# Token blocks 2 and 3 transposed on VectorE and turned through DRAM instead of on TensorE

## Chip, cores and metric

The kernel runs on one core of a Trainium2 chip. The metric is the device time of one execution in microseconds (us); the kernel before has a median of 676.11 us over three runs. Everything is float32 outside and float32r (a float32 that TensorE takes) inside, where each operand is split in a high part and the low part that the high one leaves over, and a product is summed from high x high, high x low and low x high.

## What is computed

One layer on 2048 tokens of 448 values: a layer norm, then an attention with a memory that is carried over four blocks of 512 tokens, and a gated feed-forward, both on the normalised tokens; the result is the input plus both.

```python
def _A_ref(x, wq, wk, wv, wo, beta):          # H = 16 heads of 28, N = 4 blocks of L = 512
    q, k, v = ...                             # x @ wq, x @ wk, x @ wv by heads and blocks
    for s in range(N):
        logits = jnp.einsum("bhqd,bhkd->bhqk", qs, ks) * scale + mask
        a_dot = jnp.einsum("bhqk,bhkd->bhqd", _softmax(logits), vs)
        pq = phi(qs)                          # phi(t) = t + 1 if t > 0 else exp(t)
        num = jnp.einsum("bhld,bhde->bhle", pq, M)
        den = jnp.einsum("bhld,bhd->bhl", pq, z)[..., None] + 1e-6
        outs.append(g * num / den + (1.0 - g) * a_dot)
        M = M + jnp.einsum("bhld,bhle->bhde", phi(ks), vs)
        z = z + jnp.einsum("bhld->bhd", phi(ks))
    return o @ wo

def _B_ref(x, w_gate, w_up, w_down):
    return (_sigmoid(x @ w_gate) * (x @ w_up)) @ w_down

xn = _layernorm(x)
return x + _A_ref(xn, ...) + _B_ref(xn, ...)
```

## The kernel before

The work has two stages. The **front stage** (up to about 125 us, with an overlap to 155 us) loads the four blocks of 512 tokens, normalises them, turns them so that the 448 values lie on the partitions, and computes values, keys, queries and the memory of each block. The **main stage** runs the feed-forward over 14 slices of hidden width, two at a time over all four blocks, with the attention's scores, softmax and sums woven in, and at the end the output projection. In the front stage the orders of TensorE (PE), ScalarE (ACT) and VectorE (DVE) are as the code is written; the orders of the DMA queue of SyncE (SP) and of GpSimd (POOL) are set by a scheduler. In the main stage all five are as written. Each queue is in order: what stands behind a waiting instruction waits too.

The names that matter. `acc[b]` holds the input of block b (128 tokens on the partitions, four tiles of 448): the normalisation reads it, and the main stage adds its results to it, so it is also the residual. `xs[b]` is the turned and split block, seven groups of 512 columns: groups 0 to 2 the high parts, 4 to 6 the low parts of the first 384 values, and group 3 the remaining 64 values, high in partitions 0 to 63 and low in 64 to 127. `wqk[c]` are seven chunks of the weights of keys and queries.

For each block b the loop (from `for b in range(NB)`) does this:

- **values**: four tiles `pv` of 11 matmuls (L360), copied by ScalarE to `vst` (L364), and stored to DRAM as `vd`. Behind the first tile VectorE computes the statistics of block b + 1 (L319 and on), and behind the fourth it normalises the first two tiles of that block into `xn` (L345).
- **seven chunks** of keys and queries (`keys_queries`, k = 0 to 6): 11 matmuls into the bank `pp` (L380); ScalarE copies the high part to `qk` (L381) and makes `e` from `pp` (L385, L386); VectorE makes the low part (L387) and finishes `e` (L390); SP stores `qk` to `qd` and, for queries, `e` to `fd`. Two chunks later `key_rows` transposes `e` on TensorE (`pk`, L400) into `kn`.
- **the turn of block b + 1**, a tile of 128 tokens at a time behind chunks 1 to 4 (`turn`): four transposes on TensorE into a bank `pt` (L103), the high part by ScalarE (L105), the low by VectorE (L110, L111). The other two tiles are normalised there too.
- from b = 2 on, **the recall of block b - 1**: behind the first chunk (the second in the last block) 16 small matmuls into four banks `n2` (L433), four transposes on VectorE (L439), and behind each of the next four chunks an answer: four steps on VectorE that end in the transpose into `tb` (L444), and a store from POOL's queue (`od<-tb`, L445). `tb` has two buffers.
- **update**: the memory `mst` from `kn` and `vst` (`pmm`, L411), behind the seventh chunk.

The blocks of input are loaded by SP: 0 and 1 at the start, 2 and 3 behind a chunk's store of the blocks 0 and 1 (L582). In the last block TensorE's queue mixes in the first feed-forward matmuls (`pgu`, L255). At the start of the main stage come the last recall's answers, the loads of the scores' operands (`qk<-qd`), of the unit's values (`vv`), of the weights (`raw`, which ScalarE and VectorE split into `wgu`, L93 and L94), and the additions of the down projection's banks `pd` (L181) to `acc` (L183).

Of the kernel before, what the change touches and what calls it, by code (L numbers as in the profile page):

```python
# [9 lines left out]
F32 = mybir.dt.float32  # L10
# [59 lines left out]
def kernel(  # L70
# [45 lines left out]
    def x_block(b):  # L116
        return x[b * L:(b + 1) * L, :].rearrange("(t p) d -> p t d", p=P)

    ps = ctx.enter_context(tc.tile_pool(name="psum", bufs=1, space=PSUM))
# [29 lines left out]
    vd = [dram.tile([P, NT, H * 32], F32, name=f"vd{b}") for b in range(NB)]  # L149
    od = [dram.tile([H * 32, L], F32, name=f"od{b}") for b in range(NB)]  # L150
# [23 lines left out]
    def gated():  # L174
# [49 lines left out]
        for f0 in range(0, NF, FG):  # L224
# [3 lines left out]
            if f0 == 0:  # L228
                ahead[0, 0] = lambda: (load_down(1, "raw"), ready_up(1))
                ahead[0, 2] = lambda: load_up(2)  # L230
                ahead[1, 3] = lambda: load_up(3)
# [70 lines left out]
    with tc.tile_pool(name="front", bufs=2) as sb, tc.manual_schedule(engines=FRONT):  # L302
# [40 lines left out]
        def normalise(b, t, mean, y):  # L343
# [4 lines left out]
            if b == 0:  # L348
                A.activation(xn[:, D:], xn[:, 384:D], AF.Copy)
            else:  # L350
                G.tensor_copy(xn[:, D:], xn[:, 384:D])
            return xn

# [19 lines left out]
        stored = {}  # L373

        def keys_queries(b, c):
# [12 lines left out]
            stored[b, c] = nc.sync.dma_start(qd[b][c * P:(c + 1) * P], qk.bitcast(F32)).ins  # L388
            if e is not None:
# [47 lines left out]
        def turn_back(n2, ts):  # L437
            for i in range(NG):
                V.transpose(ts[:, i, :], n2[i])  # L439
# [97 lines left out]
        for b in range(NB):  # L537
            last = b == NB - 1
            xn = {}
# [17 lines left out]
            if st and b > 0:  # L557
                st = rstd(*st)
                for n in range(2):
                    xn[n] = normalise(b + 1, n, *st[n])  # L560
            e = {}
            for k, c in enumerate((3, 4, 5, 6, 0, 1, 2) if last else range(7)):
                e[c] = keys_queries(b, c)
                if b == 0 and c + 4 < 7:
                    split_qk(c + 4)
                n = k - (1 if last else 0)
                if b > 1 and n == 0:
                    ts = kn if last else phi
                    turn_back(recall(b - 1, phi), ts)
# [10 lines left out]
                if (b, k) in ((0, 3), (1, 0)):  # L580
                    with tc.issue_after(stored[b, c]):
                        nc.sync.dma_start(acc[b + 2], x_block(b + 2))  # L582
# [18 lines left out]
                n = k - 1 if b == 0 else k + 1  # L601
                if 2 <= n < 6:
                    turn(b + 1, n - 2, xn[n - 2])
                if 0 <= n < 4 and n not in xn:
                    xn[n] = normalise(b + 1, n, *st[n])
# [298 lines left out]
```

## Time and profile before

| | us |
|---|---|
| runs | 676.11, 676.07, 677.15 |
| median | 676.11 |
| the profiled execution | 676.94 |
| its span, first to last instruction | 675.1 |
| TensorE, wait for VectorE in front of `pt` | 1.3 |
| TensorE, wait in front of `pp` | 0.9 |
| TensorE, wait in front of `pv` | 0.8 |

The profiled execution is 1.8 us longer than its span and 0.8 us longer than the median. Rows of a timeline show the start, the duration, the engine, the line of the program, the operation with what it writes and reads, and, in brackets, the time for which the engine had sat idle before it and what ended that. Neighbouring instructions of one kind are merged in a row (x11). A matmul's row overlaps the next one's, so the pace of TensorE is read from start to start.

### The profile page before, as it was taken

What the parts mean: (1) busy time and instruction counts of PE and PEld (TensorE: products, weight loads), DVE (VectorE), ACT (ScalarE), POOL (GpSimd) and SP (SyncE); (2) the same over time, 40 slices, a digit from 0 to 9 for tenths busy, and PEclk for the clock granted to TensorE, in tenths of its full rate; (3) what the DMA queues carried; (4) which work ended last, traced back from release to release, by engine and by line L of the source; (5) the groups of instructions that cost most, each with busy time, mean ns of one, the idle gap of its engine ahead of it and who ended that gap; (6) DMA issues with size and microseconds to landing.
All of it is one profiled execution on the core that took longest, in us unless ns stands there. A gap on an engine that the chain in (4) does not pass through costs nothing.

```text
span 675.1 us, 11208 instructions
## 1 busy us (share of the span) xinstructions
PE 666.7 (99%) x3954; PEld 555.1 (82%) x3954; DVE 566.2 (84%) x987; ACT 338.5 (50%) x563; POOL 141.4 (21%) x346
## 2 busy tenths in 40 slices
PE   8999999999999999999999999999999999999998
PEld 7888878778888788787887878788787887888897
DVE  6765685668989899899999889899998998999864
ACT  4846574523554564555644454465545554544320
POOL 3500010002222222142221213222222221321000
PEclk9999999999999999999999999999999999999999
DMA  7446657895423234133335422325342332423342
GB/s 272 176 162 249 211 222 260 287 290 158 126 57 102 57 102 114 52 107 88 71 66 135 103 71 57 101 58 134 81 102 57 98 81 74 101 76 81 94 165 100
DMA packets 45919, 84.42 MB, mean 125 GB/s; under 512 B 6312, under 2 KB 20520, under 8 KB 45352
## 3 DMA queue, kind: packets, MB, share of 16 engines
q1 hardware_dynamic: 42712, 76.26, 38.0%
q0 software_dynamic: 3008, 7.34, 5.1%
q8 instruction: 31, 0.51, 0.3%
q14 instruction: 24, 0.20, 0.1%
q10 hardware_dynamic: 144, 0.11, 0.0%
HBM read 51.05 MB, written 32.64 MB: 124 GB/s over the span
## 4 chain that ended last, share of the span: by engine, by line
PE 90%; issue 4%; DVE 3%; DMA 1%; ACT 1%; POOL 0%; DVEq 0%; POOLq 0%
PE pgu L255 39%; PE pd L181 20%; PE pp L380 9%; PE st L652 6%; PE pa L738 5%; PE po L837 5%; PE pv L360 4%; PE pt L103 1%; DMA od<-tb 1%; PE pk L400 1%; DVE e L390 0%; DMA acc<-in_x 0%; PE pmm L411 0%; DVE stats L319 0%; DVE qk L387 0%
## 5 line engine op out<-in xcount | busy, mean ns | idle before, releaser
L255 PE MATMUL pgu<-xs,wgu 128*128 128x512 f32 x1232 | 301.3, 392 | 0.0
L255 PEld LDWEIGHTS pgu<-xs,wgu 128*128 128x128 f32 x1232 | 228.7, 188 | 46.7 <-issue 2.5
L181 PE MATMUL pd<-wdn,hh 128*128 128x448 f32 x672 | 155.3, 366 | 0.5 <-DVE acc L183 0.5
L181 PEld LDWEIGHTS pd<-wdn,hh 128*128 128x128 f32 x672 | 122.7, 188 | 12.3 <-issue 0.8
L667 POOL TENSOR_SCALAR_AFFINE_SELECT w<-w 128x256 f32<-128x256 f32 (+1 forms) x160 | 76.1, 478 | 215.6 <-ACT w L656 149.0
L720 ACT ACTIVATE w<-w 128x1024 f32<-128x1024 f32 (+1 forms) x96 | 87.9, 915 | 58.6 <-DVE w L716 58.4
L656 ACT ACTIVATE w<-st 128x512 f32<-128x512 f32 x128 | 75.6, 592 | 55.5 <-PE st L652 51.3
L716 DVE TENSOR_TENSOR w<-w,mb 128x1024 f32<-128x1024 f32 (+1 forms) x96 | 100.7, 1056 | 0.8
L674 DVE TRANSPOSE_TENSOR_REDUCE mx<-w 128x32 f32<-128x1024 f32 x64 | 78.9, 1232 | 3.9 <-POOL w L667 3.9
L380 PE MATMUL pp<-xs,wqk 128*128 128x512 f32 x308 | 75.7, 395 | 0.9 <-DVE kn L439 0.9
L278 ACT ACTIVATE hh<-sg 128x512 fp32r<-128x512 f32 x56 | 35.4, 631 | 73.1 <-DVE sg L272 51.0
L183 DVE TENSOR_TENSOR acc<-pd,acc 128x448 f32<-128x448 f32 x112 | 67.4, 602 | 3.9 <-PE pd L181 3.9
L380 PEld LDWEIGHTS pp<-xs,wqk 128*128 128x128 f32 x308 | 56.6, 188 | 13.2 <-DVE kn L439 1.3
L652 PE MATMUL st<-qk 84*128 84x128 f32 (+3 forms) x256 | 62.2, 313 | 0.0
L652 PEld LDWEIGHTS st<-qk 84*128 84x128 f32 x256 | 47.9, 189 | 9.0 <-issue 1.4
L262 ACT ACTIVATE sg<-pgu 128x512 f32<-128x512 f32 x56 | 33.1, 592 | 39.6 <-PE pgu L255 39.6
L387 DVE TENSOR_TENSOR qk<-pp,qk 128x512 fp32r<-128x512 f32 x28 | 19.3, 689 | 33.2 <-ACT e L385 30.2
L272 DVE SCALAR_TENSOR_TENSOR sg<-sg,pgu 128x512 f32<-128x512 f32 x56 | 37.7, 673 | 9.5 <-PE pgu L255 9.3
L702 DVE STREAM_TRANSPOSE mb<-top 128x1024 f32<-128x1024 f32 x32 | 39.5, 1235 | 3.3 <-POOL top L699 3.2
L360 PE MATMUL pv<-wv,xs 128*128 128x448 f32 x176 | 37.7, 368 | 0.8 <-DVE e L390 0.5
L281 DVE SCALAR_TENSOR_TENSOR hh<-sg,hh 128x512 fp32r<-128x512 f32 x56 | 37.9, 677 | 0.3 <-ACT hh L278 0.3
L738 PE MATMUL pa<-w,vv 128*32 128x128 f32 (+3 forms) x512 | 37.8, 436 | 0.0
(100 smaller groups left out, 604.4 us busy)
## 6 DMA issues: line engine op xcount, KB each, us to landing
qk<-qd SPq DMA_DIRECT2D x192, 112.0 KB
qd<-qk SPq DMA_DIRECT2D x28, 512.0 KB
raw<-in_w_ffn SPq DMA_DIRECT2D x14, 512.0 KB
vd<-vst SPq DMA_DIRECT2D x4, 1024.0 KB
vv<-vd SPq DMA_DIRECT2D x16, 256.0 KB
od<-w POOLq DMA_DIRECT2D x16, 256.0 KB, 4.1
sums<-od SPq DMA_DIRECT2D x32, 128.0 KB
out<-acc SPq DMA_DIRECT2D x15, 224.0 KB
```

The lines of the kernel that those rows point to most:

```text
L181: T.matmul(pd[:, :D], l, r, start=n == 0, stop=n == len(mms) - 1)
L183: V.tensor_add(acc[b][:, t, :], pd[:, :D], acc[b][:, t, :])
L255: T.matmul(dst, wgu[f][:, w, side * P:(side + 1) * P], xs[b][:, a, :], start=n == 0, stop=n == len(TERMS) - 1)
L360: T.matmul(pv[:, :D], xs[b][:, a, t * P:(t + 1) * P], wv[w], start=n == 0, stop=n == len(TERMS) - 1)
L380: T.matmul(pp, wqk[c][:, w, :], xs[b][:, a, :], start=n == 0, stop=n == len(TERMS) - 1)
L652: T.matmul(st[:, at:at + L - kb * P], self.qk[:KS, 1, h, kb * P:(kb + 1) * P], self.qk[:KS, 0, h, kb * P:], start=True, stop=True)
L656: A.activation(w, st, AF.Copy)
L667: G.affine_select(d, d, pattern=pattern, base=0, channel_multiplier=-1, compare_op=ALU.is_ge, fill=MASK)
L674: V.tensor_reduce(self.mx[:, 32 * h:32 * h + 32], w3[:, h, :2 * L].rearrange("p (b n) -> p b n", n=32), axis=mybir.AxisListType.X, op=ALU. ...
L716: V.tensor_sub(w, w, m)
L720: A.activation(w, w, AF.Exp, scale=SCALE)
L738: T.matmul(pa[32 * j:32 * j + 32, kb * P:], self.vv[:, kb, 32 * j:32 * j + 32], self.pairs[j // 2].block(j % 2, kb), start=kb == 0, stop=k ...
```

## The change

Blocks 2 and 3 are no longer turned by TensorE. Their input is loaded in another layout: `load_strips` puts token 32 t + r of quarter q on partition 32 q + r, so a strip of 32 partitions holds 128 tokens in four tiles. Behind the values of block b = 1 and 2, right after the statistics, all four tiles of block b + 1 are normalised, and each is transposed by VectorE in squares of 32 x 32 into the stage, which is the buffer `acc` of the other of the two blocks (block 2 is staged in `acc[3]`, block 3 in `acc[2]`). `spread` writes the stage to a DRAM tensor `xd` by four DMAs of SP, in pieces of 128 numbers, and reads it back by two DMAs of POOL's queue: the first 384 values into the places of the low parts of `xs`, the last 64 into `tail`. `split_strips`, behind chunk k = 5, then makes the high parts on ScalarE (1536 columns and 512 columns) and the low parts on VectorE.

Since both `acc` have been used as stages, the input of blocks 2 and 3 is loaded once more in the main stage, as the residual. The load of block 3's strips moves from behind chunk 0 to behind chunk 4 of block 1.

The recall's matmuls keep their place; but the first two of the four banks are now turned by VectorE ahead of the step that finishes `e` (`between`), and the other two behind it.

```diff
+    def load_strips(b):
+        for q in range(4):
+            nc.sync.dma_start(acc[b][32 * q:32 * q + 32],
+                              x[b * L + q * P:b * L + (q + 1) * P, :].rearrange("(t r) d -> r t d", r=32))
...
+    xd = [dram.tile([D, L], F32, name=f"xd{b}") for b in range(NB)]
...
             if f0 == 0:
                 ahead[0, 0] = lambda: (load_down(1, "raw"), ready_up(1))
+                ahead[0, 3] = lambda: nc.sync.dma_start(acc[2], x_block(2))
+                ahead[1, 1] = lambda: nc.sync.dma_start(acc[3], x_block(3))
...
             if b == 0:
                 A.activation(xn[:, D:], xn[:, 384:D], AF.Copy)
+            elif b == 1:
+                G.tensor_copy(xn[:, D:], xn[:, 384:D])
             else:
-                G.tensor_copy(xn[:, D:], xn[:, 384:D])
+                s3 = stages[b].rearrange("p (i n) -> p i n", n=P)
+                V.transpose(s3[:, :, 32 * t:32 * t + 32], xn[:, :D].rearrange("p (i r) -> p i r", r=32))
             return xn
+
+        def spread(b):
+            for q in range(4):
+                nc.sync.dma_start(xd[b][:, q * P:(q + 1) * P].rearrange("(i c) n -> c i n", c=32),
+                                  stages[b][32 * q:32 * q + 32].rearrange("c (i n) -> c i n", n=P))
+            tail[b] = two_k("tail")
+            nc.gpsimd.dma_start(xs[b][:, 4:7, :].bitcast(F32), xd[b][:384].rearrange("(k p) n -> p k n", p=P))
+            nc.gpsimd.dma_start(tail[b][:64], xd[b][384:])
+
+        def split_strips(b):
+            A.activation(xs[b][:, 0:3, :], xs[b][:, 4:7, :].bitcast(F32), AF.Copy)
+            A.activation(xs[b][:64, 3, :], tail[b][:64], AF.Copy)
+            V.tensor_sub(xs[b][:, 4:7, :], xs[b][:, 4:7, :].bitcast(F32), xs[b][:, 0:3, :].bitcast(F32))
+            V.tensor_sub(xs[b][64:, 3, :], tail[b][:64], xs[b][:64, 3, :].bitcast(F32))
...
-        def keys_queries(b, c):
+        def keys_queries(b, c, between=None):
...
             stored[b, c] = nc.sync.dma_start(qd[b][c * P:(c + 1) * P], qk.bitcast(F32)).ins
+            if between:
+                between()
             if e is not None:
                 V.scalar_tensor_tensor(e, pp, 0.0, e, op0=ALU.max, op1=ALU.add)
...
-            if st and b > 0:
-                st = rstd(*st)
-                for n in range(2):
-                    xn[n] = normalise(b + 1, n, *st[n])
+                if b > 0 and t == 0:
+                    st = rstd(*st)
+                if b > 0:
+                    normalise(b + 1, t, *st[t])
+            if 0 < b < NB - 1:
+                spread(b + 1)
...
-                e[c] = keys_queries(b, c)
+                def recalled():
+                    n2.extend(recall(b - 1, phi))
+                    turn_back(n2, ts, range(2))
+
+                n2, ts = [], kn if last else phi if b > 1 else None
+                n = k - (1 if last else 0)
+                e[c] = keys_queries(b, c, recalled if b > 1 and n == 0 else None)
+                if n2:
+                    turn_back(n2, ts, range(2, NG))
...
-                if (b, k) in ((0, 3), (1, 0)):
+                if (b, k) in ((0, 3), (1, 4)):
                     with tc.issue_after(stored[b, c]):
-                        nc.sync.dma_start(acc[b + 2], x_block(b + 2))
+                        load_strips(b + 2)
...
-                n = k - 1 if b == 0 else k + 1
-                if 2 <= n < 6:
-                    turn(b + 1, n - 2, xn[n - 2])
-                if 0 <= n < 4 and n not in xn:
-                    xn[n] = normalise(b + 1, n, *st[n])
+                if b == 0:
+                    if 3 <= k:
+                        turn(1, k - 3, xn[k - 3])
+                    if 1 <= k < 5:
+                        xn[k - 1] = normalise(1, k - 1, *st[k - 1])
+                elif k == 5:
+                    split_strips(b + 1)
```

Three places of the built orders follow; the rows give the line (L), the operation, what it writes and reads, and the shape. The buffers have numbers: `xs_67` and `xs_68` are blocks 2 and 3, `xd_93` and `xd_94` the DRAM tensors that they pass through, `acc_71` and `acc_72` the inputs of blocks 2 and 3, `od_92` before and `od_96` now the stores of the first recall.

POOL's queue in the front stage, before: the copies of 64 values for the turn, and the stores of the recalled answers.

```order
L477 TENSOR_TENSOR wqk_120<-wqk_raw,wqk_120 128x512
L351 COPY xn<-xn 128x64 x9
L445 DMA od_92<-tb 128x512
L351 COPY xn<-xn 128x64
L445 DMA od_92<-tb 128x512
L351 COPY xn<-xn 128x64
L445 DMA od_92<-tb 128x512 x2
```

The same stretch of POOL's queue now:

```order
L507 TENSOR_TENSOR wqk_124<-wqk_raw,wqk_124 128x512
L359 COPY xn<-xn 128x64 x3
L371 DMA xs_67<-xd_93 128x3x512
L372 DMA tail<-xd_93 64x512
L475 DMA od_96<-tb 128x512 x3
L371 DMA xs_68<-xd_94 128x3x512
L372 DMA tail<-xd_94 64x512
L475 DMA od_96<-tb 128x512
```

Block 2 is read back with nothing ahead of it; the read of block 3 stands behind three of the four stores of the first recall's answers.

SP's queue at the start of the main stage, before (`qk_1768` and `qk_1775` are the operands of the first two pairs of heads):

```order
L634 DMA qk_1768<-qd_79 28x2x512 x6
L634 DMA qk_1775<-qd_79 28x2x512 x6
L731 DMA vv<-vd_87 128x4x128
L192 DMA raw<-in_w_ffn 128x1024
L634 DMA qk_1949<-qd_79 28x2x512 x6
```

And now:

```order
L672 DMA qk_1736<-qd_79 28x2x512 x6
L672 DMA qk_1743<-qd_79 28x2x512 x6
L769 DMA vv<-vd_87 128x4x128
L236 DMA acc_71<-in_x 128x4x448
L237 DMA acc_72<-in_x 128x4x448
L198 DMA raw<-in_w_ffn 128x1024
L672 DMA qk_1919<-qd_79 28x2x512 x6
```

The two residual loads stand ahead of a load of weights and of the third pair's operands.

VectorE's queue in the last block, around the second recall, before (`n_1495` to `n_1498` are the four banks):

```order
L387 TENSOR_TENSOR qk<-pp,qk 128x512
L390 SCALAR_TENSOR_TENSOR e<-pp,e 128x512
L439 STREAM_TRANSPOSE kn<-n_1495 128x512
L439 STREAM_TRANSPOSE kn<-n_1496 128x512
L439 STREAM_TRANSPOSE kn<-n_1497 128x512
L439 STREAM_TRANSPOSE kn<-n_1498 128x512
```

And now:

```order
L415 TENSOR_TENSOR qk<-pp,qk 128x512
L469 STREAM_TRANSPOSE kn<-n_1461 128x512
L469 STREAM_TRANSPOSE kn<-n_1462 128x512
L420 SCALAR_TENSOR_TENSOR e<-pp,e 128x512
L469 STREAM_TRANSPOSE kn<-n_1463 128x512
L469 STREAM_TRANSPOSE kn<-n_1464 128x512
```

Two of the four transposes passed the step that finishes `e`.

More of the change, by code (lines that the diff above doesn't have):

```diff
@@ L371, in values @@
             store_values(b, t, pv)
-        stored = {}
-        def keys_queries(b, c):
+        stored, tail = {}, {}
+        stages = {b: acc[k].rearrange("p t d -> p (t d)") for b, k in ((2, 3), (3, 2))}
+        def keys_queries(b, c, between=None):
             qk = four_k(F32R, "qk")
@@ L435, in recall, with turn_back @@
             return n2
-        def turn_back(n2, ts):
-            for i in range(NG):
+        def turn_back(n2, ts, groups=range(NG)):
+            for i in groups:
                 V.transpose(ts[:, i, :], n2[i])
@@ L538 @@
             last = b == NB - 1
-            xn = {}
+            xn, phi = {}, None
             if b > 1:
@@ L556 @@
                     A.activation(one, ident[:, 0:1], AF.Exp)
-            if st and b > 0:
-                st = rstd(*st)
-                for n in range(2):
-                    xn[n] = normalise(b + 1, n, *st[n])
+                if b > 0 and t == 0:
[4 more added lines that the diff above has]
+                spread(b + 1)
             e = {}
             for k, c in enumerate((3, 4, 5, 6, 0, 1, 2) if last else range(7)):
-                e[c] = keys_queries(b, c)
+                def recalled():
[6 more added lines that the diff above has]
+                    turn_back(n2, ts, range(2, NG))
                 if b == 0 and c + 4 < 7:
                     split_qk(c + 4)
[L566 to L569, printed above, removed]
                 if b > 1 and 0 < n <= NG:
```

## Prediction

> **What bounds the kernel now.** First the page: the busy shares and the chain that ended last.
>
> ```profile
> span 675.1 us, 11208 instructions
> PE 666.7 (99%) x3954; PEld 555.1 (82%) x3954; DVE 566.2 (84%) x987; ACT 338.5 (50%) x563; POOL 141.4 (21%) x346
> PEclk9999999999999999999999999999999999999999
> PE 90%; issue 4%; DVE 3%; DMA 1%; ACT 1%; POOL 0%; DVEq 0%; POOLq 0%
> ```
>
> TensorE works 99% of the span at full granted clock, so the time moves one to one with what its queue holds and with every wait put into it. Next its timeline in the front stage, blocks 1 to 3 (start, duration, instruction, idle time before it).
>
> ```profile
> 55.94 0.60 PE L103 MATMUL pt<-ident,xn 128*128 128x128 f32 x4
> 56.29 2.77 PE L380 MATMUL pp<-xs,wqk 128*128 128x512 f32 x11
> ...
> 63.08 2.78 PE L380 MATMUL pp<-xs,wqk 128*128 128x512 f32 x11
> ...
> 66.49 2.78 PE L380 MATMUL pp<-xs,wqk 128*128 128x512 f32 x11
> ...
> 69.47 2.77 PE L380 MATMUL pp<-xs,wqk 128*128 128x512 f32 x11
> ...
> 73.38 9.08 PE L360 MATMUL pv<-wv,xs 128*128 128x448 f32 x44
> ...
> 95.83 2.78 PE L380 MATMUL pp<-xs,wqk 128*128 128x512 f32 x11
> ...
> 99.49 2.75 PE L380 MATMUL pp<-xs,wqk 128*128 128x512 f32 x11
> ...
> 106.35 2.48 PE L360 MATMUL pv<-wv,xs 128*128 128x448 f32 x11
> 109.35 6.88 PE L360 MATMUL pv<-wv,xs 128*128 128x448 f32 x33 [0.52 <-DVE e L390]
> ...
> 124.40 2.77 PE L380 MATMUL pp<-xs,wqk 128*128 128x512 f32 x11 [0.86 <-DVE kn L439]
> ```
>
> TensorE hardly waits: 0.52 us at the values of block 3 and 0.86 us at its second chunk.
>
> **What goes.** A chunk with its turn (`pt`) takes 66.49 - 63.08 = 3.41 us from start to start, one without 69.47 - 66.49 = 2.98: a turn costs 0.43, and the first of a block 56.29 - 55.94 = 0.35. That is 0.35 + 3 x 0.43 = 1.64 us for the four turns of block 1. In block 2 the last turn came late as well (99.49 - 95.83 = 3.66, 0.25 more): 1.89. The 0.52 goes, since another wait will stand ahead of it. Of the 0.86, the two banks turned ahead of the `e` step bring the release forward by that step's issue interval, 123.64 - 123.03:
>
> ```profile
> 123.03 0.69 DVE L390 SCALAR_TENSOR_TENSOR e<-pp,e 128x512 f32<-128x512 f32 x1
> 123.64 2.50 DVE L439 STREAM_TRANSPOSE kn<-n 128x512 f32<-128x512 f32 x4
> ```
>
> so 0.6. Gains: 1.64 + 1.89 + 0.5 + 0.6 = **4.6 us**. VectorE and ScalarE are also rid of the splits of each turn; that shortens no row of TensorE by itself.
>
> **The new split, block 1.** The turned tokens come back whole, and ScalarE and VectorE split them in one piece of 1536 columns behind the sixth chunk. No row has that width; the nearest are
>
> ```profile
> 70.97 0.37 ACT L402 ACTIVATE kn<-pk 128x256 f32<-128x256 f32 x1
> ...
> L93 ACT ACTIVATE wgu<-raw x14: 1043/1056/1065, 106.9 to 554.3; 128x1024 fp32r<-128x1024 f32 x14
> L93 ACT ACTIVATE wdn<-rawd x13: 562/569/578, 137.7 to 560.1; 128x448 fp32r<-128x448 f32 x13
> ...
> L94 DVE TENSOR_TENSOR wgu<-raw,wgu 128x1024 fp32r<-128x1024 f32 x2 | 2.4, 1204 | 0.0
> L94 DVE TENSOR_TENSOR wdn<-rawd,wdn 128x448 fp32r<-128x448 f32 x2 | 1.2, 603 | 6.3 <-DMA qk<-qd 6.3
> ```
>
> From 448 to 1024 columns ScalarE rises by 0.487 us and VectorE by 0.601; 512 more give 1.056 + 0.43 = 1.49 and 1.204 + 0.53 = 1.74. ScalarE starts behind the last copy of `kn`, 71.34 - 1.64 = 69.7, the high half is there at 71.2, the low half at 73.0 with 0.1 for the hand-over. The values want to start at 73.38 - 1.64 = 71.74; two matmuls (0.4) need high halves only, the third the low one. Wait 73.0 - 72.1 = **0.9 us** (0.7 to 1.2 if the widths cost 0.2 less or more).
>
> That holds if the data are there by 69.7. They start early: VectorE normalises all four strips and transposes them where it now sits idle.
>
> ```profile
> 48.26 0.93 DVE L345 TENSOR_SCALAR xn<-acc,mv,y 128x448 f32<-128x448 f32 x2
> 54.76 0.69 DVE L387 TENSOR_TENSOR qk<-pp,qk 128x512 fp32r<-128x512 f32 x1 [5.57 <-ACT e L385]
> ```
>
> Four normalisations (0.5) and four transposes (0.63, the issue interval of the four in 2.50 above) end near 52.7, inside the 5.57 us. The DMA write is queued behind a 1-MB store of `vst`, for whose rate and its own the nearest row is that of the slices of 0.3 us from 144 to 156 us:
>
> ```profile
> 51.69 0.32 SPq L366 DMA_DIRECT2D vd<-vst  x1
> ...
> GB/s 382 382 379 380 362 324 407 406 408 374 347 348 346 208 122 143 130 150 116 143 116 89 143 164 157 116 102 102 109 109 143 89 61 82 328 266 212 157 219 184
> ```
>
> First stores at 380 GB/s, then short pieces at about 110. The store of `vst` is out by 55, and the 0.92 MB of tokens need 2.4 to 8.3 us: written between 59 and 65 with 1.6 us until the landing is seen (2.3 for a 256-KB store, next part, less its 0.7 at 380). The read back takes 3.7 to 7.2 us (next part): 63 to 72. I take on time, since the pieces of 512 bytes start into an empty queue.
>
> Block 3's strips, four DMAs on SP in place of one, move behind the fifth chunk's stores, some 4 us after that chunk starts at 63.08. At 380 GB/s they are in by 71 to 73; their first reader stands at 75.87 and comes no sooner, since the wait of 0.9 takes up most of block 1's 1.64. So they cost nothing; if the cover goes, each us late is one on VectorE, which then has 5 us idle.
>
> ```profile
> 75.87 0.63 DVE L319 BATCH_NORM_STATS2 stats<-acc 128x6 f32<-128x448 f32 x1
> ```
>
> **The new split, block 2.** POOL issues the read back, and in the changed order it stands behind the first three stores of the recalled answers (`od<-tb`). So it cannot start before the third `tb`, which VectorE reaches through its own queue:
>
> ```profile
> 90.01 0.69 DVE L387 TENSOR_TENSOR qk<-pp,qk 128x512 fp32r<-128x512 f32 x1
> ...
> 101.41 0.71 DVE L444 STREAM_TRANSPOSE tb<-phi 128x512 f32<-128x512 f32 x1
> ...
> 102.90 0.69 DVE L387 TENSOR_TENSOR qk<-pp,qk 128x512 fp32r<-128x512 f32 x1
> ...
> 105.31 0.71 DVE L444 STREAM_TRANSPOSE tb<-phi 128x512 f32<-128x512 f32 x1
> ...
> 102.42 0.54 POOL L445 DMA_DIRECT2D od<-tb  x1 [3.09 <-DVE tb L444]
> ...
> od<-tb POOLq DMA_DIRECT2D x2, 256.0 KB, 2.3
> DMA to landing us min/median/max: 2.3/2.8/5.8
> ```
>
> One chunk with its answer and no split of a turn lasts 3.1 us on VectorE (102.90 to 106.02). Counting from 90.01 - 0.74 (block 1's net) = 89.27, the third `tb` ends near 98.6, POOL is through its store 0.84 later (102.96 - 102.12), and the read goes out at 99.4. A 256-KB store landed after 2.3 to 5.8 us; 512 KB more take 1.4 at 380 GB/s. So 3.7 to 7.2 us; I take 4.7, nearer to the 2.3 of this very stretch, because a read competes with 770 KB of stores a chunk: landing at 104.1. [...]
>
> ScalarE could split from 101.7, so the landing decides. Low half ready: 104.1 + 1.49 + 1.74 + 0.1 = 107.5. TensorE, at the third matmul of the values: 106.35 - 0.74 - 1.89 + 0.4 = 104.1. Wait **3.4 us** (2.4 to 5.9). Queued behind the waiting ScalarE copy are chunk 7's copies; VectorE's steps of chunk 7, which free the bank of the second tile of values, end near 110, when that tile is due, so they add nothing.
>
> **The residual loaded apart.** 1.8 MB more go out on SP near 156 us, just ahead of the next weights (`raw`).
>
> ```profile
> 155.86 0.57 SPq L192 DMA_DIRECT2D raw<-in_w_ffn  x1
> ...
> 161.82 0.71 DVE L444 STREAM_TRANSPOSE tb<-kn 128x512 f32<-128x512 f32 x1 [1.90 <-DMA od<-tb]
> 163.63 0.71 DVE L444 STREAM_TRANSPOSE tb<-kn 128x512 f32<-128x512 f32 x1
> 164.26 0.58 DVE L183 TENSOR_TENSOR acc<-pd,acc 128x448 f32<-128x448 f32 x1
> ...
> 164.37 1.06 ACT L93 ACTIVATE wgu<-raw 128x1024 fp32r<-128x1024 f32 x1 [5.49 <-DVE tb L444]
> 164.90 1.48 PE L181 MATMUL pd<-wdn,hh 128*128 128x448 f32 x6 [0.53 <-DVE acc L183]
> ```
>
> This corner is tight already: a `tb` waits 1.90 us for a store, and TensorE 0.53 for the addition behind it. At 380 GB/s the new loads hold the queue 4.8 us longer. Nothing to 2.5 us; I take **0.6**, near the lower end, since TensorE itself has 1.5 us in hand at the next bank.
>
> **Sum:** -4.6 + 0.9 + 3.4 + 0.6 = **+0.3 us** on the execution profiled (676.94 us for a span of 675.1). Against the median of 676.11 that is 676.4.
>
> **Rivals.**
> - *The second turn lands in time.* If the read is in by 101.7, its wait is 0.9 like block 1's and the main loop's start has room: -4.6 + 0.9 + 0.9 = -2.8, 673.3 us. For it: the data are written by about 91. Against it: POOL's order. It needs the third answer 2.4 us earlier than VectorE's rows allow. 0.18.
> - *Slower: the residual's loads block the answers' stores.* The second store of a recalled answer after 156 lands behind 1.8 MB, the fourth `tb` waits from 163.6 to 166, and with it the addition that frees TensorE's bank: 2.5 in place of 0.6, so +2.2, 678.3. It decides if that store lands after 163.6. For it: the 1.90 above. Against: stores and loads are on two queues. 0.17.
> - *The first turn is late* (512-byte pieces at the worst rate): landing at 72 in place of 69.7 or before adds 2.3, 678.7. 0.06.
> - *The clock falls.* If the granted clock halves behind the 3.4-us wait for the next 11 matmuls, it costs another 2.7: 679.1. The row of the granted clock shows no such dip, but also no wait this long. [...] 0.04.
> - *Other*: 0.05.
>
> **How the numbers follow.** The forecast has 0.50, and its own range runs from -4.6 + 0.9 + 2.4 = -1.3 to -4.6 + 0.9 + 5.9 + 2.5 = +4.7 us. A measurement can tell 0.2%, 1.35 us, from no change. Of the 0.50, 0.02 lie below that, 0.36 within, 0.12 above. Faster: 0.18 + 0.02 + 0.02 = 0.22; same 0.38; slower 0.12 + 0.17 + 0.06 + 0.04 + 0.01 = 0.40. The range takes in the first rival and cuts the upper corner where all costs meet: 673.2 to 679.6.
>
> **What would show it.** TensorE's timeline without `pt` after 42 us and chunks of 2.98 us; a wait of about 0.9 ahead of the third matmul of block 2's values, released by VectorE's split, and one of about 3.4 in block 3's, where ScalarE's wait names the DMA into `xs`; POOL's read issued right behind the third store; 0.25 left of the 0.86; near 165 a wait of 0.5 to 1.5 on the addition. A read issued before the third store, or a split that never waits for DMA, would make it wrong.

## The result, and the profile after

The changed kernel takes **684.9 us** (median of six runs, 683.84 to 689.38), beside 677.27 for the kernel before in the same job (six runs, 676.07 to 678.65): a ratio of **1.0125**, 95% interval 1.0105 to 1.0145. It is slower, and the prediction of 676.4 (673.2 to 679.6) does not hold it. The profiled execution took 686.13 us for a span of 684.3, 9.2 more than the span before. The page of the changed kernel, its busy shares, the granted clock and the DMA engines:

```profile
span 684.3 us, 11161 instructions
PE 668.9 (98%) x3922; PEld 556.0 (81%) x3922; DVE 568.5 (83%) x983; ACT 338.6 (49%) x559; POOL 142.0 (21%) x342
PEclk9999998999999999999999999999999999999999
DMA  7448887799424332251424433323353322523342
```

TensorE has fewer instructions and yet more busy time: one slice of the clock row shows an 8, and a matmul lasts longer at a lower clock (the 11 from 81.70 us, most of them at 0.50, take 4.03 us; 11 of the shape took 2.48 at 1.00 before). In the fourth to sixth slice, 51 to 103 us, the DMA engines stand at 8, 8 and 8 tenths, where a page of the kernel before has 6, 6 and 5. TensorE's timeline of the changed kernel (start, duration, instruction, idle time before it and what ended that):

```profile
71.72 0.68 PE L387 MATMUL pv<-wv,xs 128*128 128x448 f32 x2
73.04 6.71 PE L387 MATMUL pv<-wv,xs 128*128 128x448 f32 x31 [0.64 <-DVE xs L378]
81.70 4.03 PE L387 MATMUL pv<-wv,xs 128*128 128x448 f32 x11 [1.95 <-ACT vst L391]
85.53 2.74 PE L408 MATMUL pp<-xs,wqk 128*128 128x512 f32 x11
...
106.43 1.28 PE L441 MATMUL pmm<-vst,kn 128*28 128x32 f32 x128
113.44 1.11 PE L387 MATMUL pv<-wv,xs 128*128 128x448 f32 x2 [5.72 <-ACT xs L376]
115.23 10.79 PE L387 MATMUL pv<-wv,xs 128*128 128x448 f32 x42 [0.68 <-DVE xs L378]
125.85 2.45 PE L408 MATMUL pp<-xs,wqk 128*128 128x512 f32 x10
```

Set beside the timeline before, the same places of the program stand as follows:

| place | before | after | behind by |
|---|---|---|---|
| values of block 1 | 42.04 | 42.15 | +0.1 |
| values of block 2 | 73.38 | 71.72 | -1.7 |
| first chunk of block 2 | 82.30 | 85.53 | +3.2 |
| values of block 3 due (end of `pmm`; before: their start) | 106.35 | 107.7 | +1.4 |
| first chunk of block 3 | 116.06 | 125.85 | +9.8 |
| its second chunk, behind the recall | 124.40 | 133.55 | +9.2 |
| main stage, third bank `pd` | 164.90 | 173.39 | +8.5 |
| end of the span | 675.1 | 684.3 | +9.2 |

So the gains are there (-1.8 and -1.9 in the two stretches without turns, 0.6 at the recall), and the whole loss lies in two places that took about 9 us each before: the values of block 2 lose 4.9, those of block 3 lose 8.4. All of this is the profiled execution; between the medians the loss is 7.6.

**Values of block 2.** VectorE's and ScalarE's rows show where the 1.95 comes from:

```profile
77.75 0.63 DVE L327 BATCH_NORM_STATS2 stats<-acc 128x6 f32<-128x448 f32 x1 [1.63 <-DMA acc<-in_x]
```

```profile
75.72 1.28 ACT L334 ACT_TABLE_LOAD   x1
81.01 0.20 ACT L334 ACTIVATE y<-vh 128x4 f32<-128x4 f32 x1 [4.00 <-DVE vh L329]
81.12 0.96 ACT L391 ACTIVATE vst<-pv 128x448 f32<-128x448 f32 x2
```

The strips of block 3, issued from 67.60 on, are there only at 77.7. The statistics wait 1.63 us for them, the root `y` on ScalarE waits for the statistics, and behind the root in ScalarE's queue stand the copies that free TensorE's banks of values. The last 11 matmuls then take 4.03 us. The DMA engines had no room in this stretch (length, busy time and instructions of each engine, granted clock, DMA share, GB/s); first before the change, then after:

```profile
60.00:70.00 10.00, 10.00 (x55) 8.42 (x54) 7.13 (x13) 7.87 (x16) 0.47 (x2) 1.00 0.68 258
70.00:80.00 10.00, 10.00 (x171) 8.88 (x170) 7.35 (x21) 5.49 (x10) 0.00 (x0) 1.00 0.64 227
```

```profile
60.00:70.00 10.00, 10.00 (x52) 8.26 (x51) 5.17 (x8) 7.69 (x15) 1.52 (x2) 1.00 0.96 316
70.00:80.00 10.00, 9.11 (x164) 7.28 (x162) 7.06 (x16) 5.13 (x7) 0.00 (x0) 1.00 1.00 326
```

**Values of block 3.** POOL's queue, and ScalarE at the split:

```profile
102.80 0.54 POOL L475 DMA_DIRECT2D od<-tb  x1 [2.46 <-DVE tb L474]
103.40 0.75 POOL L371 DMA_DIRECT2D xs<-xd  x1
```

```profile
111.90 1.48 ACT L376 ACTIVATE xs<-xs 128x1536 fp32r<-128x1536 f32 x1 [6.30 <-DMA xs<-xd]
```

The read goes out right behind the third store, as the order said, but it lands 8.5 us later. The stretches of the changed kernel, in the same columns:

```profile
82.00:83.00 1.00, 1.00 (x5) 0.88 (x4) 0.93 (x3) 0.98 (x2) 0.00 (x0) 0.62 0.44 123
...
84.00:85.00 1.00, 1.00 (x4) 0.87 (x3) 0.97 (x3) 0.00 (x0) 0.00 (x0) 0.50 0.46 82
85.00:86.00 1.00, 1.00 (x4) 0.86 (x4) 0.97 (x3) 0.23 (x1) 0.00 (x0) 0.67 0.01 4
...
98.00:103.00 5.00, 5.00 (x26) 4.11 (x25) 4.83 (x11) 4.06 (x8) 0.75 (x2) 1.00 0.98 383
103.00:108.00 5.00, 4.71 (x146) 3.74 (x144) 3.58 (x8) 1.99 (x4) 2.18 (x4) 1.00 0.99 285
108.00:113.00 5.00, 0.00 (x0) 0.00 (x0) 0.00 (x0) 1.10 (x1) 0.00 (x0) 1.00 0.94 328
113.00:119.00 6.00, 4.88 (x12) 3.88 (x13) 5.45 (x9) 3.45 (x7) 0.00 (x0) 0.50 0.32 125
119.00:120.00 1.00, 1.00 (x4) 0.90 (x4) 0.56 (x1) 0.54 (x1) 0.00 (x0) 0.60 0.98 256
```

Two things are to be seen. From 98 to 113 the DMA engines have no room: 0.94 to 0.99. And the granted clock falls to 0.50 at each of the two waits, for 3.4 us from 82.2 and 6.8 from 113.0 (a share of 0.62 in a microsecond is a fall 0.24 into it), so that 12 matmul records fill six microseconds. At 84 to 86 the DMA engines are busy for 0.46 and 0.01, with a clock of 0.50 and 0.67, so the slow matmuls there are not a matter of traffic. The kernel before had room from 98 to 108 us, with a share of 0.53 up to 103 and then of 0.68:

```profile
103.00:108.00 5.00, 5.00 (x146) 4.22 (x145) 4.85 (x10) 3.94 (x7) 0.54 (x1) 1.00 0.68 258
```

### The profile page after: what moved, and what is told of

It is laid out like the page before. It is cut to its first block, busy times and chain, and to the rows that moved or that the text cites. A ratio compares the mean times of both kernels' runs of the same rounds, so it can differ in the third digit from the quotient of the medians.

```text
span 684.3 us, 11161 instructions
## 1 busy us (share of the span) xinstructions
PE 668.9 (98%) x3922; PEld 556.0 (81%) x3922; DVE 568.5 (83%) x983; ACT 338.6 (49%) x559; POOL 142.0 (21%) x342
## 2 busy tenths in 40 slices
DMA packets 51295, 89.93 MB, mean 131 GB/s; under 512 B 6632, under 2 KB 25448, under 8 KB 50728
## 4 chain that ended last, share of the span: by engine, by line
PE 82%; issue 9%; DMA 4%; DVE 2%; ACT 1%; POOL 1%; SPq 0%; DVEq 0%; POOLq 0%
PE pgu L263 37%; PE pd L187 19%; PE pp L408 6%; PE st L690 5%; PE pa L776 5%; PE po L875 5%; PE pv L387 3%; DMA acc<-in_x 2%; DMA od<-w 1%; DMA od<-tb 1%; DVE stats L327 1%; DMA qd<-qk 0%; POOL od L475 0%; PE pk L430 0%; PE pt L103 0%
## 5 line engine op out<-in xcount | busy, mean ns | idle before, releaser
L387 PE MATMUL pv<-wv,xs 128*128 128x448 f32 x176 | 42.5, 397 | 9.3 <-ACT xs L376 5.7
L387 PEld LDWEIGHTS pv<-wv,xs 128*128 128x128 f32 x176 | 35.2, 206 | 14.6 <-ACT xs L376 5.8
```

Of the source, the lines that this page charges most:

```text
L387: T.matmul(pv[:, :D], xs[b][:, a, t * P:(t + 1) * P], wv[w], start=n == 0, stop=n == len(TERMS) - 1)
```

## The experiments

Twelve kernels were run. Where no other base is named, the edit is made in the changed kernel. Medians stand beside 676.65 to 677.02 for the kernel before in the same jobs; "span" is that of the profiled execution.

**1. Strips of block 3 one chunk earlier** (`e2_strips_early`).

```diff
-                if (b, k) in ((0, 3), (1, 4)):
+                if (b, k) in ((0, 3), (1, 3)):
                     with tc.issue_after(stored[b, c]):
                         load_strips(b + 2)
```

> The changed kernel, but the strips of block 3 are loaded behind chunk 3 of block 1 and not behind chunk 4. Theory 'order': they land some 3 us earlier (about 75), the statistics do not wait, the wait of 1.95 us at the fourth tile of block 2's values goes and with it the slow group behind it (1.6 us): 3 to 4 us faster. Rival 'full queue': the read back of block 2, which landed just as the split began (69.7), comes later by 1 to 3 us, and ScalarE waits there: gain under 1 us.

Median 684.66, ratio 1.0107 (1.0082 to 1.0133), span 681.4.

```profile
80.79 2.48 PE L387 MATMUL pv<-wv,xs 128*128 128x448 f32 x11 [0.34 <-ACT vst L391]
111.06 1.11 PE L387 MATMUL pv<-wv,xs 128*128 128x448 f32 x2 [5.80 <-ACT xs L376]
112.85 10.15 PE L387 MATMUL pv<-wv,xs 128*128 128x448 f32 x42 [0.68 <-DVE xs L378]
```

In the trace the cause of the 1.95 is shown: with the strips earlier 0.34 is left of it, and the 11 matmuls take 2.48 again instead of 4.03. The wait of block 3 stays. The read of block 2 lands later in this run: the wait ahead of the low parts is 1.01 in place of 0.64. In the medians the 2.9 us of the span are not to be seen; the intervals of the two ratios overlap, so the time alone does not decide between the two expectations; the trace is for the first.

**2. What the clock costs** (`e3_hold`, `e3b_hold_short`). Matmuls on the identity, whose result nobody reads, stand ahead of the values of tiles where TensorE waits; nothing is left out.

```diff
+        def hold(b, t):
+            n = {(2, 0): 3, (2, 3): 8, (3, 0): 25}.get((b, t), 0)     # e3_hold: 7, 22, 64
+            if n:
+                bk = bank("hold", "s")
+                for _ in range(n):
+                    T.matmul(bk[:, :P], ident, ident, start=True, stop=True)
...
             for t in range(3 if b == 0 else 0, NT):
+                hold(b, t)
                 values(b, t)
```

> The changed kernel with idle TensorE filled: 7, 22 and 64 matmuls of 128x128 on the identity ahead of the first and the fourth tile of block 2's values and of the first of block 3's (0.6, 2.0 and 5.8 us), whose results nobody reads. Theory 'clock': the granted clock stays at 1.00, the groups of 11 and 42 value matmuls behind the waits take 2.4 and 8.6 us in place of 4.0 and 10.8: 4 to 5 us faster, the waits for data unchanged. Rival 'contention': the matmuls are slow because of transfers into the same memory; they stay slow and nothing is gained.

> As the kernel with filled waits, but with 3, 8 and 25 idle matmuls, of 0.23 us each as that run's rows show: 0.7, 1.8 and 5.8 us, about the waits themselves. Theory 'clock': all slices at full granted clock, the value matmuls behind the waits at their old pace, and the time lower than the changed kernel's by the clock's share alone, 4 to 5 us, near 680. Rival 'contention': no gain, since the matmuls were slowed by transfers.

In the first of the two each such matmul took 0.23 us in two records (22 in 5.07 us), more than twice the 0.09 that I had taken, so the filling outlasted the waits: 695.65, ratio 1.0275 (1.0249 to 1.0302). With its waits filled the clock is 1.00 from 70 to 124 us, and the 44 matmuls of block 3's values take 9.05. Yet a later row, where TensorE is not idle, is long: 47 feed-forward matmuls from 163.73 take 12.56 us, and 10.95 in the changed kernel. That the clock fell there is my reading, from the 0.998 that this execution was granted on the mean; just ahead stand the third recall's small matmuls, whose row took 2.88 us there and 1.70 in the changed kernel:

```profile
160.93 2.88 PE L463 MATMUL n<-phi,mst 28*32 28x512 f32 x32
```

The second has the right length: median 683.64, ratio 1.0105 (1.0081 to 1.0128), span 681.1.

```profile
79.80 1.95 PE L528 MATMUL hold<-ident 128*128 128x128 f32 x16
81.50 2.45 PE L387 MATMUL pv<-wv,xs 128*128 128x448 f32 x11
...
105.82 5.85 PE L528 MATMUL hold<-ident 128*128 128x128 f32 x50
...
113.34 8.91 PE L387 MATMUL pv<-wv,xs 128*128 128x448 f32 x42 [1.12 <-DVE xs L378]
```

The waits are about as long as they were, filled, and the matmuls behind them, with a granted clock of 1.00 on the mean, take 2.45 and 8.91 in place of 4.03 and 10.79: the fallen clock is worth 1.6 + 1.9 = 3.5 us of the profiled execution, and the span is 3.2 shorter. The medians differ by 1.3, less than their intervals tell apart. The profiled execution of the changed kernel had a granted clock of 0.992, four of the other five 0.995: by that, about 11 us at half clock in the one and 7 in the others (an estimate, 2 x 0.008 and 2 x 0.005 of 684 us), so most executions lose less to the clock than the 3.5. A lower clock and slow data were two rival readings of the long matmuls; since only TensorE's idleness was taken away, it is the clock.

**3. Block 3's read ahead of the stores on POOL** (`e1_read_first`).

```diff
-            nc.gpsimd.dma_start(od[b][P * i:P * (i + 1)], tb)
+            with tc.issue_after(read[3]) if b == 1 else ExitStack():
+                nc.gpsimd.dma_start(od[b][P * i:P * (i + 1)], tb)
```

> The changed kernel, but POOL's queue has the read back of block 3 ahead of the first recall's four stores. Theory 'order': the read goes out when the tokens are written (about 94 us in place of 103.4), lands some 8 us later, before ScalarE's split can start at 105.6; the wait of 5.7 us at block 3's values falls to about 0.7 and the fall of the clock behind it (about 2.9 us) goes too: about 8 us faster than the changed kernel, near 677. Rival 'full queue': the DMA queues are busy at 0.95 and more from 90 to 112 us, so an earlier read only lands after 106 again and pushes the stores back; less than 4 us gained.

Median 681.96, ratio 1.0066 (1.0048 to 1.0085), span 679.6. VectorE and TensorE:

```profile
103.61 0.71 DVE L474 STREAM_TRANSPOSE tb<-phi 128x512 f32<-128x512 f32 x1 [4.13 <-DMA od<-tb]
```

```profile
110.21 11.29 PE L387 MATMUL pv<-wv,xs 128*128 128x448 f32 x42 [3.93 <-DVE xs L378]
```

The read goes out at 93.59 and lands before its split, and ScalarE does not wait. But the first answer's store stands behind the read, `tb` has two buffers, and the third transpose waits 4.13 us for the store; VectorE's part of the split stands behind that. A wait of 5.72 for the read has become one of 3.93 for VectorE, and the clock still falls (0.63 from 108 to 112 us, 0.52 from 112 to 116). The gain, 2.9 us between the medians, falls short of the 8 that were expected and fits the rival's number, but not its way: the read was early, and the stores were late.

**4. Strips early, and the read from ScalarE's own queue** (`e6_act_queue`): block 3's read is issued by ScalarE behind chunk 2 of block 2.

```diff
+                if (b, k) == (2, 2):
+                    read_back(3, nc.scalar)
```

> The changed kernel with strips of block 3 loaded behind chunk 3, and with the read back of block 3 issued by ScalarE's DMA queue behind chunk 2 of block 2, so that neither the answers' stores stand ahead of it nor it ahead of them. Theory 'order and shared queue': it is issued near 94 us, lands before ScalarE's split (about 103), tb never waits for a store, the wait at block 3's values falls to about 0.7 us and the clock does not fall: 9 to 12 us faster than the changed kernel, 673 to 676. Rival 'full DMA engines': the 786 KB take longer in the stretch from 94 to 104 us, whichever queue brings them; the split waits 2 us or more, or the stores of qk are late and ScalarE waits for a qk buffer: gain under 6 us.

Median 681.63, ratio 1.0067 (1.0047 to 1.0088), span 681.5. A queue of its own does not free the stores:

```profile
105.26 0.71 DVE L478 STREAM_TRANSPOSE tb<-phi 128x512 f32<-128x512 f32 x1 [2.84 <-DMA od<-tb]
```

The DMA share is 0.94 to 0.96 from 90 to 108 us. The third answer waits for a store with the read in POOL's queue (4.13 us) and with the read in ScalarE's (2.84). The gain of 3.3 us between the medians fits the rival; the read itself was in before ScalarE's split.

**5. The parts that were thought harmless.** The kernel before with the second load of `acc` added (`e7_reload_alone`), with the recall's two banks first (`e4_recall_alone`), and the changed kernel with only block 2 turned through DRAM, block 3 by TensorE (`e8_block2_only`).

```diff
+                ahead[0, 3] = lambda: nc.sync.dma_start(acc[2], x_block(2))
+                ahead[1, 1] = lambda: nc.sync.dma_start(acc[3], x_block(3))
```

> The kernel before with one part of the change alone: the inputs of blocks 2 and 3 loaded a second time at the start of the main stage (into the buffers that hold them already). Theory: nothing, at most 0.5 us. Rival of the prediction: the stores of the recalled answers land later, the wait in front of the addition grows from 0.53 to 2.5 us, 2 us slower.

678.21, ratio 1.0011 (0.9991 to 1.0030), span 675.5. The interval leaves room for a loss of up to 2.0 us, but the rival's way is not there: the wait in front of the third `pd` is 0.22, where it was 0.53.

```diff
-                    turn_back(recall(b - 1, phi), ts)
+                e[c] = keys_queries(b, c, recalled if ... else None)
+                    turn_back(n2, ts, range(2, NG))
```

> The kernel before with one part of the change alone: the first two of the four recalled banks turned ahead of the step that finishes e. Theory: the wait of 0.86 us at the second chunk of block 3 falls to about 0.2, 0.6 us faster, within what can be measured. Rival: the wait moves to a later instruction and the time stays.

676.44, ratio 0.9993 (0.9981 to 1.0005), span 674.1. The wait is 0.19 instead of 0.86, as worked out; in the time 0.6 us can't be told from nothing.

```diff
-            elif b == 1:
+            elif b != 2:
                 G.tensor_copy(xn[:, D:], xn[:, 384:D])
...
-                ahead[1, 1] = lambda: nc.sync.dma_start(acc[3], x_block(3))
```

> Half of the change: block 2 goes through VectorE and DRAM, block 3 is turned by TensorE as before, its input loaded behind chunk 3 of block 1. Theory: of the gains 1.6 (turns of block 1) and 0.6 (recall) stay, of the costs 0.7 at the first split and about 0.3 at the fourth tile; no wait long enough for the clock: 1.2 us faster than the kernel before. Rival: the costs of the changed kernel come from the traffic of either block, half of its 8 us stay.

678.22, ratio 1.0019 (1.0004 to 1.0034), span 677.3. Slower by 1.3 us (0.3 to 2.3), where 1.2 faster was expected; and one block costs far less than the rival's half of the loss.

```profile
74.00 6.71 PE L386 MATMUL pv<-wv,xs 128*128 128x448 f32 x31 [1.12 <-DVE xs L377]
81.07 2.48 PE L386 MATMUL pv<-wv,xs 128*128 128x448 f32 x11 [0.35 <-ACT vst L390]
```

Its three waits (0.48, 1.12 and 0.35) cost 2.7 us with the hand-overs, since the values and the first wait take 11.65 us (71.73 to 83.38) in place of 8.92; that is 1.1 more than the 1.7 of the four turns. The recall gives 0.65 back, and in this profile a wait of 1.7 us for ScalarE follows in front of a score (`st`), which the kernel before does not have and which was not pursued. The clock is whole at the values of block 2 (1.00 from 70 to 80 us).

**6. Full engines or a shared queue?** Half a MB of feed-forward weights, issued among block 2's stores, moved behind the fifth chunk (`e9_late_raw`); the first recall's stores issued by SP (`e10_stores_on_sp`, with the strips early); both (`e11_stores_on_sp_late_raw`).

```diff
-                if (b, k) in ((2, 1), (3, 0)):
+                if (b, k) in ((2, 4), (3, 0)):
                     with tc.issue_after(stored[b, c]):
                         next(ffn)
```

> The changed kernel with one edit: the load of 512 KB of feed-forward weights (raw), which SP issues at 94 us among block 2's stores, moves behind the fifth chunk's stores. Full DMA engines as the cause of the late landing: half a MB less ahead of block 3's read at 320 to 380 GB/s is 1.4 to 1.6 us, so the read, issued at about 103.4 behind the third store, lands 6.9 to 7.1 us later instead of 8.5, and the wait for the high parts falls from 5.7 to about 4.3; the clock may still fall. Median 683 or a little below. Fixed price of a read behind the stores of its own queue: landing stays at 8.2 to 8.5, the wait stays at 5.7, median 684.9 as before. If the weights themselves come late, ScalarE shows a wait for raw behind 113 us and TensorE one in front of the first feed-forward matmuls.

Neither: 687.3, ratio 1.0154 (1.0121 to 1.0186), span 687.7. SP issued the weights at 103.44, which is right behind POOL's read (102.77) and no longer 9 us ahead of it. ScalarE's split, and the stretch in which it waits:

```profile
114.40 1.48 ACT L376 ACTIVATE xs<-xs 128x1536 fp32r<-128x1536 f32 x1 [9.44 <-DMA xs<-xd]
```

```profile
108.00:113.00 5.00, 0.00 (x0) 0.00 (x0) 0.00 (x0) 0.00 (x0) 0.00 (x0) 0.69 1.00 328
```

The read lands 11.6 us after its issue, 3.1 more than before the edit. Three profiles with the weights ahead of the read agree on 8.4 to 8.6 (the changed kernel, the strips early, the short filling). But transfers scatter: in this same profile the read of block 2, ahead of which no order was changed, took 9.6 us in place of 8.2. And the intervals of the two ratios overlap. My expectation for full engines had the wrong sign, since I had counted the weights as ahead of the read and not asked where they would go. What this profile says: with the weights issued on another queue 0.67 us after the read, the read took 11.6 us, and 8.5 with the weights 9 us ahead of it; how much of the 3.1 is theirs is not settled.

```diff
-            nc.gpsimd.dma_start(od[b][P * i:P * (i + 1)], tb)
+            (nc.sync if b == 1 else nc.gpsimd).dma_start(od[b][P * i:P * (i + 1)], tb)
```

> Strips of block 3 loaded one chunk earlier, and the four stores of the first recall's answers issued by SP instead of POOL, so that block 3's read has POOL's queue to itself. Shared queue as the cause: the read goes out at about 93, is in by 102, and the answers' stores on SP no longer stand behind it, so the third answer buffer waits under 1.5 us instead of 4.1, the split starts near 103.2 on ScalarE and near 105 on VectorE, TensorE waits under 1 us in the values of block 3, no clock dip (42 matmuls in about 8.9), span near 674, median 675 to 677: the same as the kernel before or faster by up to 2 us. Full DMA engines as the cause: the stores land as late on SP, behind 2 MB of other stores, the third answer buffer waits 3 to 4 us again, TensorE waits 3 to 4 us and the clock falls; median 681 to 682.

> Both edits together: the answers' stores on SP, the strips one chunk earlier, and the 512 KB of weights behind the fifth chunk. Shared queue as the cause: no different from the run with the stores on SP alone, within 0.5 us. Full DMA engines as the cause: about 1.4 us less of waiting for the third answer buffer than in that run, and a median 1.4 to 3 us lower (3 if the clock's fall goes with it). If the values of block 3 then wait under 1 us, the median lies at 674.5 to 677.

Stores on SP: 679.97, ratio 1.0050 (1.0023 to 1.0078), span 678.8. Both: 679.14, ratio 1.0036 (1.0018 to 1.0054), span 675.7. The answer that waits for a buffer, on VectorE: with the stores on SP the third one does not wait and the fourth does, with both it is the third again:

```profile
101.41 0.71 DVE L474 STREAM_TRANSPOSE tb<-phi 128x512 f32<-128x512 f32 x1
...
106.56 0.71 DVE L474 STREAM_TRANSPOSE tb<-phi 128x512 f32<-128x512 f32 x1 [2.18 <-DMA od<-tb]
```

```profile
101.42 0.71 DVE L474 STREAM_TRANSPOSE tb<-phi 128x512 f32<-128x512 f32 x1 [1.26 <-DMA od<-tb]
```

Each theory seems to hold a part: the wait is 4.13 us with the stores behind the read in one queue, 2.18 on another queue, 1.26 with half a MB less in that stretch. These are single profiles, and the medians of the last two can't be told apart. With the stores on SP TensorE waits 2.22 us and the clock falls (0.73 from 108 to 113 us); the medians lie between what the two theories asked for. TensorE in the last of them waits no more than 1.31 us at one place, and its clock is 1.00 throughout:

```profile
72.84 0.68 PE L387 MATMUL pv<-wv,xs 128*128 128x448 f32 x2 [1.09 <-ACT xs L376]
74.63 6.71 PE L387 MATMUL pv<-wv,xs 128*128 128x448 f32 x31 [1.12 <-DVE xs L378]
...
108.03 4.52 PE L387 MATMUL pv<-wv,xs 128*128 128x448 f32 x20 [1.31 <-DVE xs L378]
112.81 4.67 PE L387 MATMUL pv<-wv,xs 128*128 128x448 f32 x22 [0.26 <-ACT vst L391]
```

**7. The split in groups of 512 columns** (`e12_split_by_groups`), on top of both edits.

```diff
-            A.activation(xs[b][:, 0:3, :], xs[b][:, 4:7, :].bitcast(F32), AF.Copy)
+            for g in range(3):
+                A.activation(xs[b][:, g, :], xs[b][:, 4 + g, :].bitcast(F32), AF.Copy)
...
-            V.tensor_sub(xs[b][:, 4:7, :], xs[b][:, 4:7, :].bitcast(F32), xs[b][:, 0:3, :].bitcast(F32))
+            for g in range(3):
+                V.tensor_sub(xs[b][:, 4 + g, :], xs[b][:, 4 + g, :].bitcast(F32), xs[b][:, g, :].bitcast(F32))
```

> The kernel with the answers' stores on SP, the strips early and the weights late, and in it the split of the turned block in three groups of 512 columns instead of one piece of 1536, on ScalarE (0.6 each) and VectorE (0.69 each). If what is left of the loss is the order high half, low half, then first matmuls, the first low group is ready 1.3 us after the landing instead of 3.2, the first tile of values runs beside the split, and the waits of the values of blocks 2 and 3 sum up to 1.6 to 2.0 us instead of 4.1 (1.09 + 1.12 + 0.35 + 1.31 + 0.26): profiled span near 673.5 and, where the clock stays whole, a time of 675 to 676, faster than the kernel before by 0.1 to 0.3%; median 675 to 677. If what is left is the landing itself, the waits stay within 0.5 us of 4.1 and the median at 678 to 679. In both, runs that meet a late landing lose the clock too and lie up to 4 us higher.

677.89, ratio 1.0016 (1.0002 to 1.0030), span 675.4. The granted clock is 0.999 or more in all twelve executions. The waits shrink from 4.1 to 2.6 us, not to 2.0:

```profile
75.93 0.36 PE L389 MATMUL pv<-wv,xs 128*128 128x448 f32 x1 [0.57 <-issue]
76.93 6.88 PE L389 MATMUL pv<-wv,xs 128*128 128x448 f32 x33 [0.63 <-ACT vst L393]
...
106.96 1.69 PE L389 MATMUL pv<-wv,xs 128*128 128x448 f32 x7 [0.50 <-DVE xs L380]
108.87 0.67 PE L389 MATMUL pv<-wv,xs 128*128 128x448 f32 x2 [0.23 <-DVE xs L381]
110.19 6.88 PE L389 MATMUL pv<-wv,xs 128*128 128x448 f32 x33 [0.65 <-DVE e L422]
```

Nearly all of that is at block 2 (2.56 to 1.20; at block 3 1.57 to 1.38). In this profile block 1's values start at 43.44, 1.3 later than in the changed kernel's, while the read of block 2 lands only 0.3 later than in the run with both edits; so part of the shorter wait may be that TensorE came later, and the groups' own share was not separated. The median lies in neither expected range, and its interval overlaps that of the run with both edits. Still no version with a block turned through DRAM is faster than the kernel before. A third buffer for `tb` was not tried.

## Why the prediction was wrong

Right, by its own steps: the gains of the turns (1.64 and 1.89 predicted; 1.8 and 1.9 measured), the 0.6 at the recall (0.86 to 0.20), the prices of the split (1.49 and 1.74; 1.48 to 1.49 and 1.74 to 1.76), the split behind block 1 (0.9; 0.9 from start to start, 73.04 - 71.72 less 0.4 for two matmuls), the place of the read behind the third store (103.40, where 99.4 was worked out with block 2 running 0.7 ahead and it ran 3.2 behind: 103.3). The residual's loads, 0.6 in the sum and the rival given 0.17, cost nothing that could be measured.

One of these was luck: "I take on time", for the read of block 2, which was to take 3.7 to 7.2 us because the pieces start into an empty queue. The engines were 0.96 busy from 60 to 70 us, and the read took 8.2 (61.52 to 69.7), so it landed just as ScalarE came to the split at 69.71. In the run with the late weights, where no order ahead of it was changed, it took 9.6, and TensorE waited 1.14 us for the high parts.

Wrong, three steps:

- **"So they cost nothing"**, of block 3's strips. They landed at 77.7, not at 71 to 73, and the cover that I named, VectorE's 5 idle us, was the wrong one. The instruction that holds TensorE stands on ScalarE: the root `y`, ahead of the copies of `vst`. In the values of block 2 this made 1.95 of waiting and, with the clock, 1.6 more. The run with the strips earlier takes both away.
- **"I take 4.7, nearer to the 2.3 of this very stretch"**, for the read. It took 8.5, beyond the upper bound of 7.2, and the wait was 5.72 + 0.68 in place of 3.4. The mechanism and the place were right, the term was mis-sized. I had priced a transfer at the rates of the kernel before, whose DMA engines were 53 to 68% busy there, and then added 3.7 MB to the front stage (of 5.5 in all: 84.42 MB moved before, 89.93 after; the rest is the residual's); with the engines at 0.94 to 0.99 a duration of the old trace is no price any more. For the traffic as the cause speak the full engines, the late weights (8.5 to 11.6) and, for the stores, 2.18 against 1.26, each in one profile; so the direction is supported, and the size is open. How much of the read's 8.5 is backlog and how much the short pieces was not separated.
- **The clock, given 0.04.** It fell twice, and costs 3.5 us of the profiled execution. All that I had against it was the clock row of a kernel whose longest wait in these blocks is 0.86 us. At block 2 it fell behind 1.95 us, and at block 3 at 113.0, before the first of the two matmuls that run ahead of the low parts (113.44).

By size, from the table: +0.1 - 1.8 + 4.9 - 1.9 + 8.4 - 0.6 - 0.7 + 0.7 = 9.1 of the 9.2. The 4.9 are 0.9 of split, 2.4 of the strips' wait with its hand-over, and 1.6 of clock; the 8.4 are 7.0 of waiting for read and split with the hand-overs, and 1.9 of clock, less the 0.5 that stood there before. The 0.7 gained behind the recall and lost again later (a wait of 0.76 for ScalarE at 397.70 us) was not pursued. Without the clock the loss of this execution would have been some 5.7 (an estimate, 9.2 - 3.5).

The rival's price for the clock, "another 2.7" with 11 matmuls behind the wait of block 3, was of the right order: 1.9 there, and 1.6 for the 11 of block 2.

The experiments also say why there is little to win here even when all of this is mended. Four turns cost TensorE 1.6 to 1.9 us a block. Split, landing and the queue cost that and a little more: 1.3 us net loss for one block alone, 0.16% for both with four repairs.

## What to carry to other kernels

A wait that a change may add is looked for on every engine whose queue the late instruction passes through, not only on the one that reads the data: ask what stands behind each waiting instruction, to the end of the chain. When a change adds traffic to a stretch where the DMA engines are half to two thirds busy, set the time that the added transfers hold the engines against the free share first, with short pieces at the rate that a run shows for them (from 57 to 60 us, while block 2's pieces of 512 bytes were written, 235 GB/s at a share of 0.95; from 98 to 103 us 383 at 0.98); that is what I would do now, it was not tried on another kernel. Once the stretch was full, the read took 8.5 us where I had worked out 3.7 to 7.2 from the landings of the old trace, and each new order of the queues moved the wait to whoever was next. Where TensorE runs at full clock all along, price each new wait with the fallen clock behind it as well: here 1.31 us in one piece was still free of it, 1.95 was not.

## What the runs showed of the hardware

The clock fell after less idleness than I had expected: I had given 0.04 to a fall behind a wait of 3.4 us. In the changed kernel it fell at 82.2, half a us into the matmuls behind a wait of 1.95 us, and came back at 85.7; it fell again at 113.0, in the wait of 5.72, and came back at 119.8: 3.4 us low, and 6.8, at a granted clock of 0.50. With the waits overfilled the 47 matmuls behind the small ones of 28 x 32 took 1.6 us longer than in the changed kernel (12.56 and 10.95), where no row shows TensorE idle; if that is a clock of 0.50, it was low for 3.2 us (an estimate, 2 x 1.6).

At the split of block 2 some runs lie close to each other on either side of a fall:

| waits at the values of block 2, us | behind them | clock from 70 to 80 us |
|---|---|---|
| 0.48 + 1.12 (only block 2) | 31 matmuls in 6.71 | 1.00 |
| 1.09 + 1.12 (both edits) | 31 in 6.71 | 1.00 |
| 1.14 + 1.12 (weights late) | 42 in 10.26 (8.91 at full clock) | 0.83 |
| 1.41 + 1.12 (stores on SP) | 42 in 10.26 | 0.83 |
| 1.73 + 0.91 (ScalarE's queue) | 42 in 11.15 | 0.69 |

No single number of us parts them: two waits of 2.21 in sum left the clock whole, 2.26 did not, and in the changed kernel 1.95 in one piece was enough. What parts them was not shown. The clock is a part of the scatter of the times: the kernel with both edits ran from 675.88 to 681.99 us, at granted clocks of 1.00 to 0.994. It is not the whole, since the one with shorter waits ran from 675.84 to 680.08 at 0.999 and above.
